# First batch's attention: unscaled probabilities, row factors applied to the output

## The chip, the cores and the metric

One NeuronCore of a Trainium2 chip runs the whole program. The metric is the device time of one execution in microseconds; the median of three executions of the kernel before is 1106.35 us (1105.39 to 1108.88).

## The reference

The inputs are `q`, `k`, `v` of shape (4, 8, 576, 64), a memory matrix `M_prev` and a vector `z_prev` per batch and head, a gate `beta` per head, and six feed-forward weights. For each of 4 batches and 8 heads:

```python
scores = scale * np.matmul(q, k.transpose(0, 1, 3, 2))     # causal mask follows
a = np.exp(scores - scores.max(-1, keepdims=True))
a /= a.sum(-1, keepdims=True) + 1e-09
local = np.matmul(a, v)
mem_out = einsum('bhsd,bhde->bhse', phi(q), M_prev) / (einsum('bhsd,bhd->bhs', phi(q), z_prev) + 1e-06)
out = g * mem_out + (1 - g) * local                        # g = sigmoid(beta), per head
```

The result, 2304 tokens by 512 features, goes through two feed-forward blocks: `((x@w1) * (x@w2)) @ w3 @ w_out`, and then `(sigmoid(x@w_gate) * (x@w_val)) @ w_out`. All of it is float32.

## The kernel before

**Work.** Heads go in pairs: two heads of 64 features fill the 128 partitions, four pairs (`NPAIR`) per batch. The 576 rows of a head are cut into five tiles of `T` = 116 rows. A batch's attention produces four tiles `Xt[p]` of shape 128 x 576 (features by tokens), each split into a rounded high part and a rest (`split_rows`, L310 to L313: a copy on ScalarE, a subtraction on VectorE or GpSimd). `ffn(b)` (L347) multiplies these with the weights in three-term products (`prod`, L300, matmuls at L302).

**Weights.** The weights arrive as 64-bit words and are turned into float32 on the chip, in half units of 128 x 512: `conv_step` (L180) with a scale (L199 on ScalarE or L201 on VectorE), a cast on ScalarE (L202), two integer operations on VectorE (L210, L211) and an integer add on GpSimd (L215); `split_step` (L239) then splits each half into its two parts (L311, L313) into a ring of `RING` = 5 slots. `w3` and `w_out` are first multiplied with each other (`prep`, L315: the `wps` matmuls).

**Stages.** The first stage runs attention of batch 0 beside the first four weight products (`start`, L781). `ffn(0)` follows, with attention of batch 1 woven in, and needs `Xt[0]` to `Xt[3]` for its `ab` matmuls; then `ffn(1)`, `ffn(2)` and `ffn(3)`, each with the attention of the next batch.

**Order.** `drive` (L750) takes one piece of attention for each piece of weight work by their costs. In the first stage only SyncE's queue has an order written by hand (L803); on the other engines a planner that simulates the time line at build time orders the instructions, with attention ahead by a priority of 400 (`AHEAD`). From `ffn(0)` on TensorE's order is the written one too (L814).

**Attention of batch 0, one pair.** For each row tile `i`: `s_part` makes the scores (L552) and VectorE adds the mask and takes the minimum (L557); `e_part` (L568) does the exponential on ScalarE with the row sum as a second result (L572, shown as the helper's L105); `n_part` (L577) adds 1e-9 to the two sums (L580), takes reciprocals (L581), and multiplies each head's probabilities by reciprocal and `1 - g` (L583; in batch 0 always on GpSimd, by `SHARE_N`). `t_part` (L595) transposes the result on TensorE against the identity (L613) and copies it out of PSUM (L629 or L631), three tiles behind (`LAG0`). `mem_steps` (L485) makes the scaled `phi(q)` (`mphi`; L495 and L504 on GpSimd), `qt_part` (L634) transposes it (L640, copies L646). `a_part` (L658) accumulates in one PSUM tile `o`: first the memory matrix times `qts` (L666), then the values times the transposed probabilities (L674, L681). `l_part` (L688) calls `tail` (L444), which splits the PSUM tile directly into `Xt[p]` while `xfree` is set, which holds for batch 0.

**PSUM.** `ps_f` has three buffers, shared by the feed-forward and weight products, by `qts` and by the wide transposes; `o` has one.

Of the kernel before, what the change touches and what calls it, by code (L numbers as in the profile page):

```python
# [7 lines left out]
F32 = mybir.dt.float32  # L8
# [42 lines left out]
def tile_attention_memory_ffn(  # L51
# [31 lines left out]
    idf = cp.tile([128, 128], F32, name="idf")  # L83
    idr = cp.tile([128, 128], F32R, name="idr")
    msk = cp.tile([T, SP], F32, name="msk")
# [363 lines left out]
    def attention(b, lag):  # L449
# [73 lines left out]

        sp = {}
        ots = {}
        qts = {}
        np_ = {"n": 0}

        def s_part(p, i, n):
            w = T * (i + 1)  # L530
            if n == 0:
                ps_ = []
                for hh in range(2):
                    name = f"p{b}_{p}_{i}_{hh}"
                    if first and np_["n"] % 2 == 0:
                        m = np_["n"] // 2 % P0
                        ps_.append(fp.tile([T, 2 * S], F32, tag=f"h{m}", name=name, bufs=1)[:, :SP])
                    else:
                        ps_.append(ap.tile([T, SP], F32, tag="p", name=name, bufs=PB))
                    np_["n"] += 1  # L540
                sp[p, i] = (ps_, ap.tile([T, 8], F32, tag="sm", name=f"sm{b}_{p}_{i}", bufs=6))
            ps_, sm = sp[p, i]
            c0, c1 = (0, w) if w <= 512 else ((0, SP // 2), (SP // 2, SP))[n]
# [24 lines left out]
        def e_part(p, i, hh):  # L568
            w = T * (i + 1)
            n = 1 if w > 512 else 0  # L570
            ps_, sm = sp[p, i]
            act_fn(  # L572
                out=ps_[hh][:, :w], in_=ps_[hh][:, :w], func=AF.Exp, scale=-1.0,
                bias=sm[:, 2 * hh + n : 2 * hh + n + 1], accum_out=sm[:, 4 + hh : 5 + hh],
            )

        def n_part(p, i):  # L577
            w = T * (i + 1)
            ps_, sm = sp[p, i]
            nc.vector.tensor_scalar(sm[:, 4:6], sm[:, 4:6], 1e-9, None, ALU.add)  # L580
            nc.vector.reciprocal(sm[:, 6:8], sm[:, 4:6])  # L581
            for hh in range(2):
                lower(SHARE_N).tensor_scalar(  # L583
                    ps_[hh][:, :w], ps_[hh][:, :w], sm[:, 6 + hh : 7 + hh],
                    omg[:T, 2 * p + hh : 2 * p + hh + 1], ALU.mult, ALU.mult,
                )
# [47 lines left out]
        def qt_part(p):  # L634
            qt = ap.tile([128, SP], F32, tag="qt", name=f"qts{b}_{p}")
            if first:
                for ts_ in (range(3), range(3, NT)):
# [7 lines left out]
                    w = T * len(ts_)  # L645
                    nc.scalar.copy(qt[:, ts_[0] * T : ts_[0] * T + w], ps[:, :w])  # L646
            else:
                ot = ps_o.tile([128, 1024], F32, tag="o", name=f"qt{b}_{p}")
# [9 lines left out]
        def a_part(p, part):  # L658
            X = 2 * T
            v_, m_ = pairs[p][1], pairs[p][2]  # L660
            halves_ = [slice(64 * hh, 64 * hh + 64) for hh in range(2)]
            if part == 0:
                ots[p] = ps_o.tile([128, 1024], F32, tag="o", name=f"o{b}_{p}")
# [7 lines left out]
            for j in range(2) if part == 0 else range(2, NT):  # L671
                if j < 2:
                    for hh, r in enumerate(halves_):
                        nc.tensor.matmul(  # L674
                            ot[r, XO + j * T : 512], v_[:, j, hh],
                            pq[:, hh, 2 * j : j + 2].rearrange("p a c -> p (a c)"),
                            start=False, stop=j == 1,
                        )
                q0 = max(2, j) * T
                for hh, r in enumerate(halves_):  # L680
# [3 lines left out]
                        if j < 4 else pt[:, hh, 3, 0, : S - 4 * T],  # L684
                        start=False, stop=j == NT - 1,
                    )

        def l_part(p):  # L688
            ot = ots.pop(p)[:, XO : XO + S]
            if state["xfree"]:  # L690
                tail(b, p, ot)
            else:
                xp = ap.tile([128, S], F32, tag="xp", name=f"xp{b}_{p}", bufs=4)
                nc.scalar.copy(xp, ot)
# [74 lines left out]
    def setup():  # L769
# [4 lines left out]
        nc.sync.dma_start(out=idf, in_=ident)  # L774
        nc.scalar.copy(idr, idf)
        nc.scalar.activation(out=g, in_=bt, func=AF.Exp, scale=-1.0)
# [110 lines left out]
```

## Time and profile before

| | us |
|---|---|
| median of three executions | 1106.35 |
| the profiled execution, its own time | 1107.55 |
| its span, first to last instruction | 1105.8 |
| TensorE busy | 1063.3 (96%) |
| VectorE busy | 533.9 (48%) |
| ScalarE busy | 468.7 (42%) |
| GpSimd busy | 326.9 (30%) |

The busy shares are means over stages with different limits. The batches after the first stage differ much from it: TensorE is busy throughout from 400 us on, while VectorE, ScalarE and GpSimd have most of their work before that. The change touches only what runs before about 128 us, so the views are read for that stretch. In the rows below PE is TensorE's matmul, PEld its weight load, DVE VectorE, ACT ScalarE, POOL GpSimd. The span starts 1.75 us short of the execution's own time.

### The profile page before, as it was taken

What the parts mean: (1) busy time and instruction counts of PE and PEld (TensorE: products, weight loads), DVE (VectorE), ACT (ScalarE), POOL (GpSimd) and SP (SyncE); (2) the same over time, 40 slices, a digit from 0 to 9 for tenths busy, and PEclk for the clock granted to TensorE, in tenths of its full rate; (3) what the DMA queues carried; (4) which work ended last, traced back from release to release, by engine and by line L of the source; (5) the groups of instructions that cost most, each with busy time, mean ns of one, the idle gap of its engine ahead of it and who ended that gap; (6) DMA issues with size and microseconds to landing.
All of it is one profiled execution on the core that took longest, in us unless ns stands there. A gap on an engine that the chain in (4) does not pass through costs nothing.

```text
span 1105.8 us, 19723 instructions
## 1 busy us (share of the span) xinstructions
PE 1063.3 (96%) x7616; PEld 950.7 (86%) x7616; DVE 533.9 (48%) x1251; ACT 468.7 (42%) x1030; POOL 326.9 (30%) x260
## 2 busy tenths in 40 slices
PE   6989798999999899999999999999999999999998
PEld 3555586887999789898999899889999899999998
DVE  7995888758788734553222415544222402212210
ACT  6776565645655633554322424454222412212210
POOL 5887565625666532222000202321000200000000
PEclk9999889999999899999999999999999999999999
DMA  8565568856888556443545454423554355454451
GB/s 271 167 207 186 178 219 287 272 188 211 268 298 305 206 193 220 149 151 128 171 156 171 153 171 159 163 85 134 163 167 160 101 164 189 154 171 171 154 174 61
DMA packets 69238, 201.76 MB, mean 182 GB/s; under 512 B 9624, under 2 KB 15896, under 8 KB 69144
## 3 DMA queue, kind: packets, MB, share of 16 engines
q1 hardware_dynamic: 69144, 200.50, 55.2%
q8 instruction: 60, 0.98, 0.4%
q14 instruction: 34, 0.28, 0.1%
HBM read 160.10 MB, written 40.37 MB: 181 GB/s over the span
## 4 chain that ended last, share of the span: by engine, by line
PE 75%; DVE 13%; POOL 4%; issue 4%; ACT 3%; DMA 2%; SPq 0%; DVEq 0%; POOLq 0%; ACTq 0%
PE gv L302 21%; PE ab L302 18%; PE ot L302 13%; PE xw L302 7%; PE s L552 4%; PE t L613 4%; DVE wraw L211 3%; PE o L681 3%; PE wps L302 3%; DVE wraw L210 2%; POOL wraw L215 2%; DVE p L557 1%; PE o L666 1%; POOL wslot L313 1%; DMA k<-wslot 1%
## 5 line engine op out<-in xcount | busy, mean ns | idle before, releaser
L302 PE MATMUL gv<-x,wslot 128*128 128x288 f32 x2304 | 308.2, 295 | 3.9 <-DVE hgraw L417 2.6
L302 PEld LDWEIGHTS gv<-x,wslot 128*128 128x128 f32 x2304 | 305.8, 188 | 5.8 <-DVE hgraw L417 4.2
L302 PE MATMUL ab<-x,wslot 128*128 128x288 f32 x1536 | 231.7, 303 | 0.0
L302 PEld LDWEIGHTS ab<-x,wslot 128*128 128x128 f32 x1536 | 210.6, 191 | 11.5 <-issue 8.3
L302 PE MATMUL ot<-hg,wslot 128*128 128x288 f32 x1152 | 166.1, 301 | 4.1 <-DVE hg L313 3.8
L583 POOL TENSOR_SCALAR p<-p,sm,omg 116x116 f32<-116x116 f32 (+4 forms) x100 | 100.6, 1010 | 224.2 <-DVE sm L581 159.8
L302 PEld LDWEIGHTS ot<-hg,wslot 128*128 128x128 f32 x1152 | 156.5, 190 | 10.4 <-issue 4.6
L215 POOL TENSOR_TENSOR wraw<-wraw,cr 128x512 int32<-128x512 int32 x76 | 112.1, 1489 | 65.7 <-DVE wraw L211 56.6
L105 ACT ACTIVATE p<-p,sm 116x116 f32<-116x116 f32 (+4 forms) x160 | 92.9, 582 | 73.4 <-DVE sm L557 68.5
L557 DVE CUSTOM_DVE_ANT_0 p<-s,msk 116x116 f32<-116x116 f32 (+4 forms) x160 | 68.2, 453 | 108.5 <-PE s L552 108.3
L417 DVE TENSOR_TENSOR hgraw<-gv,gsb 128x288 f32<-128x288 f32 x96 | 43.7, 455 | 141.5 <-PE gv L302 134.1
L302 PE MATMUL xw<-h,wslot 128*128 128x288 f32 x768 | 111.4, 299 | 0.2 <-DVE h L313 0.2
L302 PEld LDWEIGHTS xw<-h,wslot 128*128 128x128 f32 x768 | 103.1, 188 | 3.8 <-issue 2.5
L105 ACT ACTIVATE gsb<-gv 128x288 f32<-128x288 f32 x96 | 39.4, 410 | 112.0 <-PE gv L302 112.0
L613 PE MATMUL t<-idf,p 116*116 116x116 f32 x480 | 70.1, 276 | 14.0 <-DVE p L583 9.6
L613 PEld LDWEIGHTS t<-idf,p 116*116 116x116 f32 x480 | 54.8, 140 | 28.7 <-issue 16.5
L495 POOL TENSOR_TENSOR me<-mphi,z 116x640 f32<-116x640 f32 x16 | 25.4, 1589 | 176.0 <-issue 174.5
L373 DVE TENSOR_TENSOR hraw<-ab,asb 128x288 f32<-128x288 f32 x64 | 29.1, 456 | 70.1 <-PE ab L302 66.9
L202 ACT ACTIVATE cr<-r 128x512 int32<-128x512 uint32 x76 | 51.4, 676 | 27.0 <-POOL wraw L215 26.9
L211 DVE SCALAR_TENSOR_TENSOR wraw<-cy,wraw 128x512 int32<-128x512 int32 x76 | 62.3, 843 | 0.2
L313 POOL TENSOR_TENSOR wslot<-wraw,wslot 128x512 fp32r<-128x512 f32 x36 | 50.6, 1405 | 29.4 <-ACT wslot L311 28.8
L311 ACT CAST hg<-hgraw 128x576 fp32r<-128x576 f32 x48 | 32.3, 672 | 57.5 <-DVE hgraw L417 57.5
(79 smaller groups left out, 1139.0 us busy)
## 6 DMA issues: line engine op xcount, KB each, us to landing
wslot<-k SPq DMA_DIRECT2D x180, 512.0 KB, 3.6
k<-wslot SPq DMA_DIRECT2D x60, 512.0 KB, 5.6
r<-in_gv_dram SPq DMA_DIRECT2D x24, 512.0 KB, 4.9
qk<-in_qk_dram SPq DMA_DIRECT2D x32, 290.0 KB, 4.1
r<-in_w3t_dram SPq DMA_DIRECT2D x16, 512.0 KB, 4.0
r<-in_w_dram SPq DMA_DIRECT2D x16, 512.0 KB, 4.6
r<-in_o_dram SPq DMA_DIRECT2D x12, 512.0 KB, 5.4
qnr<-in_qn_dram SPq DMA_DIRECT2D x16, 320.0 KB, 3.3
```

Source lines behind the costliest of these rows:

```text
L105: ins = nc.scalar.activation(**kw)
L202: nc.scalar.activation(out=r, in_=w[:, :, 0].bitcast(U32), func=AF.Copy, scale=2.0**-29)
L211: nc.vector.scalar_tensor_tensor(z, y, -(2**31), z, ALU.bitwise_and, ALU.bitwise_or)
L215: nc.gpsimd.tensor_tensor(z, z, tmp["r"], ALU.add)
L302: nc.tensor.matmul(ps, w[:, wi, blk, :], x[:, xi, cols : cols + n], start=first and part == 0, stop=last and part == 2,)
L313: eng.tensor_sub(dst[:, 1], src, dst[:, 0].bitcast(F32))
L417: nc.vector.tensor_mul(hraw[:, c0 : c0 + HS], pss[1][:, :HS], asb)
L552: nc.tensor.matmul(os_[hh], q_[r, 0, i * T : (i + 1) * T], k_[r, 1, c0:c1], start=x == 0, stop=x == len(terms) - 1,)
L557: nc.vector.tensor_tensor_reduce(out=ps_[hh][:, c0:c1], in0=os_[hh], in1=msk[:, SP - w + c0 : SP - w + c1], scale=-0.125, scalar=3.0e38 if ...
L583: lower(SHARE_N).tensor_scalar(ps_[hh][:, :w], ps_[hh][:, :w], sm[:, 6 + hh : 7 + hh], omg[:T, 2 * p + hh : 2 * p + hh + 1], ALU.mult, ALU ...
L613: nc.tensor.transpose(tp[:T, c : c + T], src[hh][:, j * T : (j + 1) * T], idf[:T, :T])
L681: nc.tensor.matmul(ot[r, XO + q0 : XO + S], v_[:, j, hh], pt[:, hh, j].rearrange("p a c -> p (a c)")[:, q0 - X : S - X] if j < 4 else pt[: ...
```

## The change

In batch 0 the probabilities are transposed and used without their row factor. The ten row sums of a pair are collected in one small tile, get one addition and one reciprocal per pair, and are spread on GpSimd to a 116 x 640 tile that holds, for each row, the factor `(1-g)/sum` repeated over the head's 64 features. TensorE multiplies this with the identity (a transposition), ScalarE copies the result out of PSUM, VectorE multiplies the pair's output `o` with it, GpSimd adds the memory part, and `tail` splits the sum, now from SBUF. The memory part is no longer accumulated in `o`: `qt_part` multiplies `qts` by the memory matrix in two column halves through `ps_f`, and ScalarE copies the product over `qts`. An unused constant `idr` goes. The other batches keep their order of work.

```diff
-    idr = cp.tile([128, 128], F32R, name="idr")
@@ e_part
-                bias=sm[:, 2 * hh + n : 2 * hh + n + 1], accum_out=sm[:, 4 + hh : 5 + hh],
+                bias=sm[:, 2 * hh + n : 2 * hh + n + 1],
+                accum_out=sums[p][:, i, hh : hh + 1] if first else sm[:, 4 + hh : 5 + hh],
@@ n_part
+            if first:
+                if i == NT - 1:
+                    sums_ = sums[p]
+                    nc.vector.tensor_scalar(sums_, sums_, 1e-9, None, ALU.add)
+                    nc.vector.reciprocal(sums_, sums_)
+                    r = ap.tile([T, NT, 2, D], F32, tag="xp", name=f"spread{p}", bufs=4)
+                    nc.gpsimd.tensor_mul(
+                        r, sums_.unsqueeze(3).to_broadcast([T, NT, 2, D]),
+                        omg[:T, 2 * p : 2 * p + 2].unsqueeze(1).unsqueeze(3).to_broadcast([T, NT, 2, D]),
+                    )
+                    spread[p] = r.rearrange("p t a d -> p t (a d)")
+                return
@@ qt_part
+                m_ = pairs[p][2]
+                for c0, c1 in ((0, HS), (HS, S)):
+                    ps = ps_f.tile([128, 512], F32, tag="f", name=f"m{b}_{p}_{c0}")
+                    for hh in range(2):
+                        r = slice(64 * hh, 64 * hh + 64)
+                        nc.tensor.matmul(ps[r, :HS], m_[r], qt[r, c0:c1], start=True, stop=True)
+                    nc.scalar.copy(qt[:, c0:c1], ps[:, :HS])
@@ a_part
-            if part == 0:
+            if part == 0 and first:
+                ots[p] = ps_o.tile([128, 1024], F32, tag="o", name=f"o{b}_{p}")
+            elif part == 0:
...
-                            start=False, stop=j == 1,
+                            start=first and j == 0, stop=j == 1,
@@ l_part
-            if state["xfree"]:
+            if first:
+                x = ap.tile([128, NT * 2 * D], F32, tag="xp", name=f"xs{p}", bufs=4)[:, :S]
+                for ts_ in (range(2), range(2, NT)):
+                    c0, c1 = ts_[0] * T, min(S, (ts_[-1] + 1) * T)
+                    ps = ps_f.tile([128, 512], F32, tag="f", name=f"r{p}_{c0}")
+                    for n, t in enumerate(ts_):
+                        nc.tensor.matmul(
+                            ps[:, n * T : (n + 1) * T], spread[p][:, t], idf[:T, :T], start=True, stop=True
+                        )
+                    nc.scalar.copy(x[:, c0:c1], ps[:, : c1 - c0])
+                nc.vector.tensor_mul(x, ot, x)
+                nc.gpsimd.tensor_add(x, x, qts[p][:, :S])
+                tail(b, p, x)
+            elif state["xfree"]:
                 tail(b, p, ot)
@@ setup
-        nc.scalar.copy(idr, idf)
```

## Rows read from the trace of the kernel before

**Rows 1.** Stretches (us): busy time of PE, PEld, DVE, ACT, POOL; clock; DMA share, GB/s.

```profile
8.00:85.00 77.00, 68.84 (x277) 36.95 (x279) 72.54 (x169) 59.98 (x140) 64.03 (x54) 1.00 0.67 215
85.00:108.00 23.00, 22.68 (x127) 12.60 (x124) 15.07 (x48) 16.54 (x42) 17.93 (x18) 1.00 0.52 163
108.00:128.00 20.00, 20.00 (x108) 14.77 (x107) 14.01 (x25) 12.19 (x25) 10.60 (x10) 1.00 0.62 204
128.00:140.00 12.00, 2.64 (x15) 1.68 (x14) 12.00 (x24) 5.33 (x13) 7.04 (x6) 0.65 0.58 174
140.00:424.00 284.00, 268.99 (x1913) 242.42 (x1912) 201.98 (x399) 157.21 (x321) 152.79 (x109) 0.97 0.73 246
```

**Rows 2.** Chain of waits, 0 to 108 us, shares by engine and line.

```profile
by line: PE s L552 11.2%; DVE wraw L211 11.1%; PE wps L302 9.8%; DVE wraw L210 7.8%; DVE p L557 7.6%; PE t L613 5.7%; DMA r<-in_wo_dram 4.6%; issue 3.6%; POOL p L583 3.6%; DVE mphi L493 3.0%; POOL wraw L215 2.9%; PE o L681 2.5%; DVE wslot L
```

**Rows 3.** Groups by line, 0 to 108 us: busy us, mean ns | idle before, releasers.

```profile
L583 POOL TENSOR_SCALAR p<-p,sm,omg 116x116 f32<-116x116 f32 (+4 forms) x39 | 35.3, 913 | 17.9 <-DVE sm L581 17.3 <-ACT pt L631 0.6
L580 DVE TENSOR_SCALAR sm<-sm 116x2 f32<-116x2 f32 x20 | 5.7, 285 | 6.1 <-ACT p L105 6.1
L581 DVE RECIPROCAL sm<-sm 116x2 f32<-116x2 f32 x20 | 3.2, 158 | 0.3
L313 DVE TENSOR_TENSOR x<-o,x 128x576 fp32r<-128x576 f32 x3 | 2.2, 748 | 0.0
```

**Rows 4.** Same view: the operations nearest to those added.

```profile
L495 POOL TENSOR_TENSOR me<-mphi,z 116x640 f32<-116x640 f32 x4 | 6.2, 1550 | 0.8 <-DVE sm L580 0.8
L504 POOL TENSOR_TENSOR mphi<-mphi,mn 116x640 f32<-116x640 f32 x4 | 5.6, 1400 | 0.3 <-DVE sm L581 0.2 <-DVE mn L500 0.2
L640 PE MATMUL qt<-idf,mphi 116*128 116x116 f32 x20 | 3.4, 308 | 0.0
L646 ACT COPY qts<-qt 128x348 f32<-128x348 f32 (+1 forms) x8 | 2.8, 388 | 0.0
```

**Rows 5.** Same view: VectorE's SBUF work beside GpSimd's.

```profile
L215 POOL TENSOR_TENSOR wraw<-wraw,cr 128x512 int32<-128x512 int32 x20 | 28.8, 1452 | 5.2 <-DVE wraw L211 3.4 <-DVE sm L581 1.8
L211 DVE SCALAR_TENSOR_TENSOR wraw<-cy,wraw 128x512 int32<-128x512 int32 x20 | 20.1, 1011 | 0.2
L210 DVE TENSOR_SCALAR wraw<-cy 128x512 int32<-128x512 int32 x20 | 12.7, 644 | 0.2
L493 DVE SCALAR_TENSOR_TENSOR mphi<-qnr,me 116x640 f32<-116x640 f32 x4 | 5.3, 1332 | 0.0
```

**Rows 6.** By tile and by line: shortest/median/longest ns of those three VectorE groups.

```profile
L211 DVE SCALAR_TENSOR_TENSOR wraw<-cy,wraw x76: 666/682/1772, 9.7 to 388.4; 128x512 int32<-128x512 int32 x76
...
L210 DVE TENSOR_SCALAR wraw<-cy x76: 401/416/1744, 8.6 to 386.7; 128x512 int32<-128x512 int32 x76
...
L493 DVE SCALAR_TENSOR_TENSOR mphi<-qnr,me x4: 798/1400/1733, 10.7 to 90.3; 116x640 f32<-116x640 f32 x4
```

**Rows 7.** Time line, VectorE and GpSimd: start us, us, operation [idle before].

```profile
118.24 1.28 POOL L313 TENSOR_TENSOR wo<-wraw,wo 128x512 fp32r<-128x512 f32 x1 [0.43 <-ACT wo L311]
118.28 1.27 DVE L498 TENSOR_SCALAR mn<-mn 116x10 f32<-116x10 f32 x1
...
16.82 0.16 DVE L498 TENSOR_SCALAR mn<-mn 116x10 f32<-116x10 f32 x1
```

**Rows 8.** Time line, VectorE: additions that waited for an exponential.

```profile
89.52 0.47 DVE L580 TENSOR_SCALAR sm<-sm 116x2 f32<-116x2 f32 x1 [1.89 <-ACT p L105]
...
92.67 0.73 DVE L580 TENSOR_SCALAR sm<-sm 116x2 f32<-116x2 f32 x1 [0.82 <-ACT p L105]
```

**Rows 9.** Time line: the end of the first stage, last tail and first `ab` product.

```profile
121.55 0.64 ACT L311 CAST x<-o 128x576 fp32r<-128x576 f32 x1 [1.51 <-PE o L681]
...
125.18 3.01 PE L302 MATMUL wps<-wo,wslot 128*128 128x512 f32 x12
...
126.83 0.75 DVE L313 TENSOR_TENSOR x<-o,x 128x576 fp32r<-128x576 f32 x1
...
128.03 0.56 PE L302 MATMUL ab<-x,wslot 128*128 128x288 f32 x3
```

More of the change, by code (lines that the diff above doesn't have):

```diff
@@ L524, in attention @@
         sp = {}
+        sums = {}
+        spread = {}
         ots = {}
@@ L541, in s_part @@
                 sp[p, i] = (ps_, ap.tile([T, 8], F32, tag="sm", name=f"sm{b}_{p}_{i}", bufs=6))
+                if first and i == 0:
+                    sums[p] = ap.tile([T, NT, 2], F32, tag="sums", name=f"sums{p}", bufs=2)
             ps_, sm = sp[p, i]
@@ L684, in a_part @@
                         if j < 4 else pt[:, hh, 3, 0, : S - 4 * T],
-                        start=False, stop=j == NT - 1,
+                        start=first and j == 0, stop=j == NT - 1,
                     )
@@ L689, in l_part @@
             ot = ots.pop(p)[:, XO : XO + S]
-            if state["xfree"]:
+            if first:
[12 more added lines that the diff above has]
+            elif state["xfree"]:
                 tail(b, p, ot)
             else:
-                xp = ap.tile([128, S], F32, tag="xp", name=f"xp{b}_{p}", bufs=4)
+                xp = ap.tile([128, NT * 2 * D], F32, tag="xp", name=f"xp{b}_{p}", bufs=4)[:, :S]
                 nc.scalar.copy(xp, ot)
```

## The prediction, made before the change was run

> **What bounds the kernel now.** I read the stretches first, cut where the character of the work changes. From 8 to 85 us VectorE is busy 72.54 of 77 us, GpSimd 64.03, ScalarE 59.98; from 85 to 128 us the matmul row is full instead, and VectorE has idle time (15.07 of 23, 14.01 of 20) [rows 1]. A full matmul row overstates TensorE, since matmuls overlap, but nothing else in that stretch is close to full. Behind it lies a hole: between 128 and 140 us TensorE works 2.64 of 12 us while VectorE works all 12, and the granted clock of that stretch is 0.65, a mean between its two levels of 1.2 and 2.4 GHz. The stretch from 140 to 424 us, the rest of `ffn(0)`, is not touched by the change; what is gained or lost by 128 us is carried into it, if nothing swallows it on the way.
>
> The chain of waits to 108 us says the same: no line has more than 11.2%, and VectorE's weight conversions (L211, L210) and score step (L557) stand beside TensorE's scores, weight products and transpositions. GpSimd's scaling, the work that is removed, has 3.6% of 108 us there, 3.9 us [rows 2], though it is GpSimd's largest group with 35.3 us [rows 3]. So most of what goes was off the path, and the gain has to come from VectorE and from waits.
>
> **What goes, by engine.** GpSimd: 39 recorded scalings, 35.3 us. VectorE: 20 additions and 20 reciprocals, 5.7 + 3.2 = 8.9 us [rows 3]. The four `o` products with the memory matrix are moved, not removed. ScalarE loses one copy of 0.3 us at start-up, which I count as nothing.
>
> **What comes.** Per pair, VectorE gets one addition and one reciprocal on 116 x 10; I take the means of the 116 x 2 forms, since so few columns cost mostly the start: 4 x (0.285 + 0.158) = 1.8 us. It gets one multiplication of 128 x 576 out of PSUM; the tail's subtraction has that shape and source, 0.748 us: 4 x 0.748 = 3.0 us [rows 3]. The tail's subtraction now reads SBUF alone; I leave its time unchanged. VectorE's own sum: 1.8 + 3.0 - 8.9 = -4.1 us.
>
> GpSimd gets four spreading multiplications (nearest: L495, 1.55 us) and four additions of 128 x 576 (nearest: L504, 1.40 us) [rows 4]: 11.8 us. Its load falls by 23.5 us. In itself that is worth nothing where GpSimd isn't last.
>
> TensorE gets 20 transpositions of the shape of L640, 3.4 us in all [rows 4]; the moved products keep their columns. ScalarE gets 16 copies like L646, 16 x 0.388 = 6.2 us. It was busy 59.98 of 77 us, so the copies are hidden behind VectorE there; were that cover gone, three pairs' share, 4.7 us, would be paid. SyncE's queue gets no DMA and keeps its order; the memory matrix is read a little earlier, but the load of `v`, which stands ahead of it in that queue, is released as before.
>
> **Where the two engines meet.** The trace shows VectorE held up while GpSimd works: an addition on 116 x 10 took 1.27 us beside a GpSimd subtraction of 1.28 us, and 0.16 us elsewhere [rows 7]. Three VectorE groups of the first 108 us, held against their shortest run, lost 20 x (1.011 - 0.666) + 20 x (0.644 - 0.401) + 4 x (1.332 - 0.798) = 6.9 + 4.9 + 2.1 = 13.9 us [rows 5, 6]. Beside them GpSimd's four large groups worked 35.3 + 28.8 + 6.2 + 5.6 = 75.9 us [rows 3 to 5], so VectorE lost 0.18 us per us of GpSimd work. By that rate the removed scalings gave back 6.4 us and the new ones cost 2.1 us. But on the time line the long VectorE runs lie mostly beside GpSimd's two-input operations, and the scalings have one input. I take half of the credit: 2.1 - 3.2 = -1.1 us. The ends: full credit, -4.3 us; no credit and every new GpSimd operation holding up VectorE for the 1.27 - 0.16 = 1.11 us of rows 7, +8.9 us.
>
> The Trainium skill, "SBUF — State Buffer", section "SBUF: two separate sides", calls this an exclusive lock on a port pair, held for a whole instruction, and has VectorE lose it when it reads two SBUF tensors or runs in its two-port mode. By it the scalings would have locked like the rest, so the credit would be whole; but the same rule speaks against the change, since the new GpSimd operations lock as well and the tail's subtraction now reads two SBUF tensors. The pair of rows at 118 us agrees with it.
>
> **The sum.** VectorE: -4.1 - 1.1 = -5.2 us over four pairs. Three pairs lie where VectorE is full, -3.9 us. After 85 us TensorE is full: it gets two pairs' transpositions, +1.7 us. There, VectorE waited twice in its queue with an addition for an exponential, 1.89 and 0.82 us [rows 8], with the next tile's score step behind it, on which that tile's exponential and then TensorE wait; those additions are gone: -2.7 us. What is late next there is TensorE's own order.
>
> The last pair's end grows. Before, the output goes to a ScalarE copy at 121.55 and a VectorE subtraction at 126.83 that ends 127.58, while TensorE has 24 weight products to do until 128 and then starts `ab` [rows 9]: the tail had 0.45 us to spare. After, a VectorE product (0.75) and a GpSimd addition (1.40) come in between, in queues that also hold conversions: a subtraction or conversion behind them waits too. Without delay in a queue it ends earlier than the old one; with the old delay of 4.6 us it ends 2.1 us later, less the spare 0.45. I take +1.0 us between 0 and 1.7.
>
> Together: -3.9 + 1.7 - 2.7 + 1.0 = -3.9 us, against the profiled execution's own 1107.55 us (its span of 1105.8 and 1.75 around it). The median, 1106.35, lies 1.2 us lower; I forecast for it: 1106.35 - 3.9 = 1102.5 us, 0.35% less. About 0.3%, 3.3 us, is what a measurement of this kernel can tell from no change, so this forecast lies at that edge.
>
> **Rivals.** *GpSimd was the real bound.* With full credit VectorE's sum is -4.1 - 4.3 = -8.4, three quarters -6.3, and the total -6.3 + 1.7 - 2.7 + 1.0 = -6.3. If TensorE's waits behind the scaling also matter, the chain's 3.9 us [rows 2] go in addition: -10.2 us, 1096.1. For: GpSimd was busy 64.03 of 77 us [rows 1], and the scaling stood between each exponential and its transpositions. Against: GpSimd itself waited 17.3 us for VectorE's reciprocals [rows 3].
>
> *The locks eat it.* In the stretch to 85 us, six of the eight new two-input GpSimd operations each start just ahead of a VectorE operation. No credit, 8.9 us of cost: VectorE -4.1 + 8.9 = +4.8, three quarters +3.6; and the waits of rows 8 stay, now behind locks: 3.6 + 1.7 + 1.0 = +6.3 us, 1112.7. It decides from about 1.3 us of lock wait per pair more than before, where the total crosses zero (-3.9 against 3 x 1.3). For: rows 7, and that GpSimd keeps a full queue of conversions. Against: eight operations beside 28 of that kind that were there before [rows 4, 5] and cost VectorE far less each. By the rule of the Trainium skill named above, this price would be paid by each VectorE operation that loses the lock, and the removed ones would pay theirs back.
>
> *The hole swallows it.* From 128 to 140 us VectorE is full and TensorE waits [rows 1]. If the hole's end hangs on VectorE's conversions, and those on DMA and ring slots rather than on the first stage, `ab` starts earlier only to wait longer: -3.9 becomes about -1 us, 1105.3. For: TensorE idles 9.4 us there. Against: every conversion is issued behind the same queue and would move with it.
>
> *The planner reorders.* The first stage's order comes from a simulation at build time, so the new instructions can shift others: a weight product of 3.0 us [rows 9] put before a score step or after it. One such shift either way, +-3 us, is in the range.
>
> **Chances.** Forecast (between -2 and -6 us) 0.40, of which a little over half lies beyond 3.3 us; GpSimd the bound 0.22; locks 0.20; hole 0.14; that the engines don't do what the change says, with the order so altered that none of these fits, 0.04. Faster by over 0.3%: 0.22 + 0.23 + 0.02 = 0.47. Slower by over 0.3%: 0.20 + 0.02 and 0.01 of the hole's, 0.23. Within: 0.30. The range reaches from GpSimd's case, 1096.1, less 1 for its scatter, to just under the locks' full price: 1095 to 1112.
>
> **What would show it.** Right: GpSimd's busy time in the first stage falls by about 23 us, VectorE's by about 5; L211's and L210's means fall a little; the first `ab` product starts near 124 instead of 128 us; from 140 us on everything is shifted alike. Wrong: L211 or L210 longer on average than 1.011 and 0.644 us (locks); the first `ab` product earlier by 8 us or more (GpSimd); the shift present at the first `ab` product and gone at 140 us (hole); the first `ab` product late, with TensorE waiting for the last tail's GpSimd addition, which would make the +1.0 term wrong.

## The result and the profile after

The kernel after takes **1112.96 us** (median of 5; 1110.49 to 1114.84), the kernel before 1106.35: a ratio of 1.0054 [1.0033, 1.0074]. It is slower, by 6.6 us; the forecast was 1102.5 us, and the time lies 1 us above the range. The profiled execution took 1110.49 us (span 1108.7), against 1107.55 (1105.8) before, so the profile shows 2.9 of the 6.6 us.

The stretches of the kernel after, in the columns of [rows 1]:

```profile
8.00:85.00 77.00, 72.00 (x288) 37.83 (x289) 72.72 (x150) 63.44 (x152) 44.96 (x32) 1.00 0.67 222
85.00:108.00 23.00, 22.69 (x122) 13.83 (x122) 13.52 (x35) 15.15 (x37) 10.27 (x8) 1.00 0.39 127
108.00:128.00 20.00, 19.16 (x111) 14.01 (x110) 11.28 (x22) 11.77 (x28) 9.36 (x8) 1.00 0.49 163
128.00:140.00 12.00, 9.02 (x39) 6.49 (x39) 12.00 (x20) 5.34 (x12) 8.38 (x6) 0.86 0.56 166
140.00:424.00 284.00, 265.05 (x1889) 238.01 (x1890) 210.28 (x410) 159.69 (x327) 156.08 (x112) 0.98 0.74 248
```

To 85 us GpSimd's busy time falls as forecast, from 64.03 to 44.96 us with new work in it, but VectorE's does not fall at all (72.54 to 72.72); it falls from 85 to 128 us, by 4.28 us, part of which is work that now comes after 128 us. From 128 to 140 us TensorE, which waited there before, has 9.02 us of work, most of it work that was done by 128 us before. The lateness is still there at the first `xw` matmul of `ffn(0)` (the product that follows `ab`), before and after:

```profile
245.76 0.56 PE L302 MATMUL xw<-h,wslot 128*128 128x288 f32 x3
```

```profile
249.81 0.56 PE L301 MATMUL xw<-h,wslot 128*128 128x288 f32 x3
```

In all 20 profiles of this study the end of the span follows the first `xw` matmul by 858.5 to 860.3 us, so what a variant does to the time is settled in the first 250 us.

The groups of 0 to 108 us that answer to [rows 4, 5]; L210, L209, L214, L494 are L211, L210, L215, L495 of before, L592 makes the spread factors, L729 adds the memory part:

```profile
L210 DVE SCALAR_TENSOR_TENSOR wraw<-cy,wraw 128x512 int32<-128x512 int32 x20 | 20.6, 1038 | 0.2
...
L214 POOL TENSOR_TENSOR wraw<-wraw,cr 128x512 int32<-128x512 int32 x20 | 28.8, 1443 | 28.8 <-DVE wraw L210 18.8 <-DVE mn L498 6.8 <-ACT cr L201 1.4
L209 DVE TENSOR_SCALAR wraw<-cy 128x512 int32<-128x512 int32 x20 | 14.6, 738 | 0.3 <-ACT cy L198 0.2
...
L494 POOL TENSOR_TENSOR me<-mphi,z 116x640 f32<-116x640 f32 x4 | 6.3, 1585 | 2.6 <-DVE mphi L492 2.6
L592 POOL TENSOR_TENSOR spread<-sums,omg 116x640 f32<-116x640 f32 x4 | 5.6, 1397 | 1.5 <-DVE sums L590 1.1 <-ACT qts L672 0.4
...
L729 POOL TENSOR_TENSOR xs<-xs,qts 128x576 f32<-128x576 f32 x2 | 3.0, 1480 | 2.9 <-DVE xs L728 2.8
```

The means that should have fallen rose, 1011 to 1038 and 644 to 738 ns, and GpSimd now waits 18.8 us for L210 (3.4 us before). A weight product is here one PSUM tile `wps` of 12 matmuls (the prediction calls a single matmul so). The first stage makes eight of them, two in each of the four steps of `start`: the first pass, with the first half of `w_out`; the second pass, with the second half, follows in `ffn(0)`. On TensorE's time line the end of the stage, which answers to [rows 9], looks like this: first the 8th product of before, then the kernel after, with VectorE's last tail put between.

```profile
115.84 3.02 PE L302 MATMUL wps<-wo,wslot 128*128 128x512 f32 x12
```

```profile
120.60 7.20 PE L301 MATMUL wps<-wo,wslot 128*128 128x512 f32 x29
...
123.79 0.76 DVE L312 TENSOR_TENSOR x<-xs,x 128x576 fp32r<-128x576 f32 x1 [2.25 <-ACT x L310]
...
127.99 0.97 PE L301 MATMUL wps<-wo,wslot 128*128 128x512 f32 x3 [0.19 <-POOL wo L312]
...
130.30 0.50 PE L301 MATMUL wps<-wo,wslot 128*128 128x512 f32 x1 [1.34 <-DVE wo L312]
...
133.29 3.42 PE L301 MATMUL wps<-wo,wslot 128*128 128x512 f32 x12
...
136.55 0.56 PE L301 MATMUL ab<-x,wslot 128*128 128x288 f32 x3
```

The last tail is ready at 124.55 us, 3 us earlier than before. But the 7th and 8th weight products, done by 118.9 us before, start at 120.60, when attention is over; the second half of `w_out`, whose buffers they hold, is converted only behind them, and TensorE waits for it at 127.99 and 130.30. The first `ab` starts at 136.55 instead of 128.03 us. Part of that is given back in the hole, which VectorE's conversions fill in both kernels; 4.0 us are left at `xw`. The start of `ab` alone doesn't tell the time of a variant: in z_wo_before (point 6), which is faster than the kernel before, it lies at 138.53 us.

### The profile page after: what moved, and what is told of

The parts are those of the page before. It is cut to its first block, busy times and chain, and to the rows that moved or that the text cites. A ratio compares the mean times of both kernels' runs of the same rounds, so it can differ in the third digit from the quotient of the medians.

```text
span 1108.7 us, 19741 instructions
## 1 busy us (share of the span) xinstructions
PE 1071.8 (97%) x7656; PEld 956.0 (86%) x7656; DVE 538.6 (49%) x1223; ACT 473.9 (43%) x1045; POOL 303.6 (27%) x228
## 4 chain that ended last, share of the span: by engine, by line
PE 73%; DVE 15%; issue 4%; DMA 3%; ACT 3%; POOL 2%; SPq 0%; POOLq 0%; DVEq 0%; ACTq 0%
PE gv L301 21%; PE ab L301 18%; PE ot L301 13%; PE xw L301 7%; PE s L555 4%; DVE wraw L210 3%; PE t L631 3%; PE o L709 3%; DVE wraw L209 3%; DVE p L560 2%; DMA k<-wslot 2%; DVE wslot L312 2%; DVE cy L200 1%; PE wps L301 1%; PE o L694 1%
## 5 line engine op out<-in xcount | busy, mean ns | idle before, releaser
L214 POOL TENSOR_TENSOR wraw<-wraw,cr 128x512 int32<-128x512 int32 x76 | 113.2, 1502 | 90.7 <-DVE wraw L210 68.6
L601 POOL TENSOR_SCALAR p<-p,sm,omg 116x116 f32<-116x116 f32 (+4 forms) x60 | 63.5, 1058 | 196.8 <-DVE sm L599 131.4
L494 POOL TENSOR_TENSOR me<-mphi,z 116x640 f32<-116x640 f32 x16 | 25.6, 1597 | 177.1 <-issue 174.5
L210 DVE SCALAR_TENSOR_TENSOR wraw<-cy,wraw 128x512 int32<-128x512 int32 x76 | 62.3, 843 | 0.2
L310 ACT CAST hg<-hgraw 128x576 fp32r<-128x576 f32 x48 | 32.4, 674 | 57.5 <-DVE hgraw L416 57.5
```

Of the source, the lines that this page charges most:

```text
L210: nc.vector.scalar_tensor_tensor(z, y, -(2**31), z, ALU.bitwise_and, ALU.bitwise_or)
L214: nc.gpsimd.tensor_tensor(z, z, tmp["r"], ALU.add)
L601: lower(SHARE_N).tensor_scalar(ps_[hh][:, :w], ps_[hh][:, :w], sm[:, 6 + hh : 7 + hh], omg[:T, 2 * p + hh : 2 * p + hh + 1], ALU.mult, ALU ...
```

## The experiments

All ratios are to the kernel before on the same chip, with 95% intervals; half widths of differences are the root of the summed squares. The kernels come in the order in which the reasons were taken apart.

**1. The removal alone, and the change without its spread factors.** x_rem is the kernel before with

```diff
 def n_part(p, i):
+    if first:
+        return
```

and x_nospread the kernel after with

```diff
-                    r = ap.tile([T, NT, 2, D], F32, tag="xp", name=f"spread{p}", bufs=4)
-                    nc.gpsimd.tensor_mul(
...
-                for ts_ in (range(2), range(2, NT)):
...
-                    nc.scalar.copy(x[:, c0:c1], ps[:, : c1 - c0])
-                nc.vector.tensor_mul(x, ot, x)
+                nc.vector.tensor_copy(x, ot)
```

> The kernel before with batch 0's additions, reciprocals and scalings left out and nothing in their place (batch 0 is not normalised): what the removal alone is worth. Order theory (the loss is that the planner puts the last two weight products behind the last attention work, plus TensorE's share of the new products): without new work the removal gains, 1099 to 1104 us, first ab product near 124 us. Rival, the removal is worth nothing because GpSimd and VectorE's small operations were hidden: 1105 to 1108 us.

> The changed kernel without the row factors (no spreading on GpSimd, no 20 products and 8 copies; VectorE copies o instead of multiplying it; batch 0 is not normalised): the memory part alone in its new place. TensorE theory (the 20 factor products cost 5.6 us of TensorE at two passes each, and push the last weight products behind): 1102 to 1106 us. Lock theory (new two-input GpSimd operations hold VectorE up): half of them stay, so about half of the loss, 1109 to 1110 us.

Measured: x_rem 1105.08 us, **0.9974 [0.9958, 0.9990]**; x_nospread 1106.00 us, 0.9988 [0.9977, 0.9999]. Taking the whole scaling away, with nothing in its place, is worth 2.9 us at this interleaving. The stretch from 8 us to the first weight product of the second pass, before and in x_rem:

```profile
8.00:121.45 113.45, 104.98 (x475) 59.24 (x475) 95.07 (x232) 84.76 (x199) 89.01 (x78) 1.00 0.64 207
```

```profile
8.00:120.30 112.30, 108.80 (x474) 62.13 (x473) 83.02 (x189) 84.24 (x198) 52.10 (x38) 0.97 0.62 201
```

VectorE's two conversion groups in x_rem, 0 to 108 us:

```profile
L211 DVE SCALAR_TENSOR_TENSOR wraw<-cy,wraw 128x512 int32<-128x512 int32 x20 | 15.6, 789 | 0.2
L210 DVE TENSOR_SCALAR wraw<-cy 128x512 int32<-128x512 int32 x20 | 12.2, 616 | 0.0
```

VectorE gives back 12.05 us (95.07 to 83.02) and GpSimd 36.9, and the stage ends 1.15 us earlier. Of VectorE's time 5.0 us come from the conversions themselves (20.1 to 15.6 and 12.7 to 12.2, against [rows 5]): the removed scalings did hold it up. What closes is TensorE's idle time, 8.47 to 3.50 us. Its row gets 3.8 us longer with the same products, and the granted clock of the stretch is 0.97, by estimate (3% of 112.3 us) 3.4 us of full-speed time lost. So VectorE's load did not set the length of this stage, at this interleaving: after 12 us of relief TensorE's row is nearly all of it, in part at the lower clock. x_rem was run at one interleaving only, and point 4 shows how much that choice weighs; what the removal is worth at another is not known.

**2. Multiplications or products?** Of the 6.6 us, x_nospread leaves none, so in this interleaving they come with the spread factors: four large GpSimd multiplications, or the factor products with their copies, and the order planned for either. v_one makes the factors once, for one query tile, in one small multiplication of 0.46 us:

```diff
-                    r = ap.tile([T, NT, 2, D], F32, tag="xp", name=f"spread{p}", bufs=4)
-                    nc.gpsimd.tensor_mul(
...
+                    if not spread:
+                        spread["r"] = ap.tile([T, 2 * D], F32, tag="spc", name="spread", bufs=1)
+                        nc.gpsimd.tensor_mul(
...
-                            ps[:, n * T : (n + 1) * T], spread[p][:, t], idf[:T, :T], start=True, stop=True
+                            ps[:, n * T : (n + 1) * T], spread["r"], idf[:T, :T], start=True, stop=True
```

v_mul has the second half of x_nospread's edit, from `for ts_` on, and keeps the multiplications.

> The kernel after, with the spread factors made once, from the first pair's sums and for one query tile, and used for all pairs and tiles: the row factors of all other tiles are left out. 20 factor products per batch, their copies and VectorE's product stay, and TensorE's planned order is the one of after but for two score steps; three of the four large GpSimd multiplications, 4.2 us, and their hold on VectorE are gone. If the GpSimd multiplications and their locks are the loss: 1106 to 1109 us (0.998 to 1.002), as x_nospread. If the factor products with the order that goes with them are: 1110 to 1114 us (1.003 to 1.007).

> The reverse: the kernel after with all four GpSimd spreading multiplications but without the factor products, their ScalarE copies and the row factors on the output (a plain copy takes the place of VectorE's product; the normalisation is left out). TensorE's planned order is nearly that of x_nospread. If the locks are the loss: 1110 to 1114 us (1.003 to 1.007). If the factor products with their order are: 1105 to 1108 us (0.998 to 1.001).

Measured: v_one 1109.34 us, **1.0020 [1.0008, 1.0032]**; v_mul 1108.76 us, **1.0015 [1.0003, 1.0026]**. Neither theory has it alone. The multiplications cost 0.27% (+-0.16) without the products and 0.34% (+-0.24) with them; the products with what comes along cost 0.32% (+-0.16) and 0.39% (+-0.24). Each alone they make 0.59%, together 0.66%, so the two nearly add up. VectorE's conversions, 0 to 108 us, in x_nospread, v_mul, v_one and x_frac125 (point 4: all of the change, woven otherwise):

```profile
L210 DVE SCALAR_TENSOR_TENSOR wraw<-cy,wraw 128x512 int32<-128x512 int32 x20 | 18.1, 912 | 0.2
L209 DVE TENSOR_SCALAR wraw<-cy 128x512 int32<-128x512 int32 x20 | 13.5, 686 | 0.6 <-ACT cy L198 0.6
```

```profile
L210 DVE SCALAR_TENSOR_TENSOR wraw<-cy,wraw 128x512 int32<-128x512 int32 x20 | 19.6, 989 | 0.2
L209 DVE TENSOR_SCALAR wraw<-cy 128x512 int32<-128x512 int32 x20 | 14.0, 706 | 0.4 <-ACT cy L198 0.4
```

```profile
L210 DVE SCALAR_TENSOR_TENSOR wraw<-cy,wraw 128x512 int32<-128x512 int32 x20 | 19.1, 958 | 0.2
L209 DVE TENSOR_SCALAR wraw<-cy 128x512 int32<-128x512 int32 x20 | 13.9, 702 | 1.4 <-POOL wslot L312 0.9 <-ACT cy L198 0.5
```

```profile
L210 DVE SCALAR_TENSOR_TENSOR wraw<-cy,wraw 128x512 int32<-128x512 int32 x20 | 18.8, 946 | 0.2
L209 DVE TENSOR_SCALAR wraw<-cy 128x512 int32<-128x512 int32 x20 | 13.6, 689 | 1.2 <-ACT cy L198 0.8 <-POOL wslot L312 0.3
```

With the multiplications L210 and L209 take 19.6 + 14.0 us instead of 18.1 + 13.5 (2.0 more, v_mul), and in after 20.6 + 14.6 instead of 19.1 + 13.9 (2.2 more than v_one). In this interleaving 4 to 6 us of two-input GpSimd work go with about 2 us more on VectorE, some 0.4 to 0.5 us per us, where the 35.3 us of scalings cost these groups 5.0 us, 0.14 per us. That is no price of the operation: x_frac125 has the same instructions as after, with three of the four multiplications, 3.8 us, before 108 us, and its two groups take 18.8 + 13.6 us, 2.8 less than after and 0.8 more than x_nospread, 0.2 us per us. How long VectorE is held up depends on what the order puts beside what, and no run shows how much of the multiplications' 0.3% is hold-up and how much is order.

**3. TensorE's own time for the products.** x_tr makes each factor product a transposition; y_tr125 does so at the interleaving of 1.25 of point 4.

```diff
-                        nc.tensor.matmul(
-                            ps[:, n * T : (n + 1) * T], spread[p][:, t], idf[:T, :T], start=True, stop=True
-                        )
+                        nc.tensor.transpose(ps[:, n * T : (n + 1) * T], spread[p][:, t], idf[:T, :T])
```

> The changed kernel with the 20 factor products issued as transpositions, one pass each, nothing else. TensorE theory: 10 passes per pair become 5, 2.8 us of TensorE in all, so 1110 us; if only the order counts, it is as the changed kernel, 1112 to 1113 us, since the planned order still has the last two weight products at the end. Lock theory: 1112 to 1113 us.

> The changed kernel at 1.25 with the 20 factor products as transpositions: does TensorE's extra work count once the order is mended? If it does, 2.8 us less of it give 1103 to 1105 us against 1106.3 without; if VectorE or its queue sets the end of the stage, 1105 to 1107 us.

Measured: x_tr 1114.11 us, 1.0056 [1.0040, 1.0072]; y_tr125 1.0013 [1.0003, 1.0023], against 0.9994 for its own pair x_frac125. The groups of products on TensorE, 0 to 121 us: the memory products of before, then after and x_tr:

```profile
L666 PE MATMUL o<-qts,ms 64*64 64x232 f32 (+1 forms) x32 | 6.2, 493 | 0.0
```

```profile
L671 PE MATMUL m<-qts,ms 64*64 64x288 f32 x32 | 7.4, 492 | 0.0
L724 PE MATMUL r<-idf,spread 116*128 116x116 f32 x40 | 6.4, 291 | 0.0
```

```profile
L724 PE MATMUL r<-idf,spread 116*128 116x116 f32 x20 | 3.7, 281 | 0.2 <-POOL p L601 0.2
```

A factor product leaves two records where the transposition leaves one, and they take 6.4 us instead of 3.7. The moved memory products take 7.4 us instead of 6.2. In the row of the stretch up to the second pass they show: the kernel after has 112.24 us of it busy, 7.26 more than before, and 2.51 us less idle, which is the 4.75 us by which its second pass starts later.

```profile
8.00:126.20 118.20, 112.24 (x512) 64.98 (x513) 95.71 (x205) 89.08 (x213) 62.80 (x45) 1.00 0.59 193
```

Yet halving the records gains nothing that shows: x_tr stands 0.02% (+-0.26) above after, which alone would hardly exclude a gain of 2.7 us (0.24%), but y_tr125 is 0.19% (+-0.13) slower than its pair. So TensorE's time for them alone hardly accounts for what they cost; the copies on ScalarE and the order are left, and no run decides between these. In x_tr's profile the clock was also at its lower level within the first stage, so this one profile can't be read as a pure saving of 2.7 us.

**4. The order.** The planner weaves weight products and attention by costs; the factor of the first stage, 1.0, sets how far attention may run ahead.

```diff
-    drive(start(), chain(a0, atts[1]), 42.4 * NPREP + 8 * WAIT, ATOT, 1.0, most=9)
+    drive(start(), chain(a0, atts[1]), 42.4 * NPREP + 8 * WAIT, ATOT, 1.25, most=9)
```

x_frac125 and v_f11 (1.1) are the kernel after, y_bfrac125 and y_bfrac09 (0.9) the kernel before.

> The changed kernel with one number of the interleaving altered (the share by which attention runs ahead of the weight products in the first stage, 1.0 to 1.25): the same instructions, the last weight products now planned beside attention, none behind it. Order theory: first ab product back near 128 us, 1102 to 1107 us. TensorE theory and lock theory: the same work and the same locks, 1111 to 1114 us.

> The kernel after, whole, with the interleaving factor of the first stage at 1.1, between 1.0 (1.0054) and 1.25 (0.9994); the planned order has the 7th weight product ahead of the last output products and the 8th behind. If the loss grows with how far the weight products fall behind attention: between the two, 1107 to 1112 us (1.000 to 1.005). If the order does not decide: as after, 1111 to 1114 us.

> The kernel before with the same altered number of the interleaving, 1.25: the control. Order theory, strict form (the change itself is worth about nothing or a small gain, and its loss comes from where the last weight products stand): the order of before was already good, so this stays within 1104 to 1108 us. Rival, 1.25 is simply a better number for any kernel and hides a real loss of the change: 1100 to 1103 us.

> The kernel before with that number at 0.9: nothing of the change in it, but the last weight product and most of the one ahead of it now planned behind the last attention work. Order theory: slower by most of the change's loss, 1109 to 1113 us, first ab product after 132 us. If the change's own instructions make its loss: 1105 to 1108 us.

Measured: x_frac125 1106.32 us, **0.9994 [0.9985, 1.0002]**; v_f11 1.0037 [1.0019, 1.0054], between, but not told apart from after; y_bfrac125 0.9998 [0.9987, 1.0009]; y_bfrac09 1116.28 us, **1.0091 [1.0074, 1.0108]**. The same instructions as in after, woven otherwise, lose nothing; and the kernel before, with nothing of the change, loses more than the change does when its weight products are pushed back. TensorE's weight products at the end of the stage, y_bfrac09 and then x_frac125:

```profile
125.55 5.63 PE L302 MATMUL wps<-wo,wslot 128*128 128x512 f32 x22
131.36 0.96 PE L302 MATMUL wps<-wo,wslot 128*128 128x512 f32 x3 [0.18 <-POOL wo L313]
...
133.67 0.50 PE L302 MATMUL wps<-wo,wslot 128*128 128x512 f32 x1 [1.34 <-DVE wo L313]
...
139.98 0.56 PE L302 MATMUL ab<-x,wslot 128*128 128x288 f32 x3
```

```profile
109.66 3.02 PE L301 MATMUL wps<-wo,wslot 128*128 128x512 f32 x12
...
114.80 3.04 PE L301 MATMUL wps<-wo,wslot 128*128 128x512 f32 x12
...
124.08 2.33 PE L301 MATMUL wps<-wo,wslot 128*128 128x512 f32 x9
...
130.59 0.56 PE L301 MATMUL ab<-x,wslot 128*128 128x288 f32 x3
```

y_bfrac09 shows the picture of after, down to the waits of 0.18 and 1.34 us for `w_out`. In x_frac125 the 7th and 8th products run at 109.66 and 114.80 us, before the last outputs; the second pass starts at 124.08 and has no wait. The stretches of x_frac125 to its second pass and on to its first `xw`, then the second of these in after:

```profile
8.00:124.08 116.08, 108.99 (x513) 63.97 (x513) 100.71 (x211) 90.88 (x219) 66.45 (x47) 0.97 0.64 208
124.08:244.68 120.60, 111.42 (x725) 94.26 (x725) 94.20 (x205) 68.54 (x149) 64.91 (x48) 0.93 0.71 233
```

```profile
126.20:249.81 123.61, 111.06 (x725) 92.36 (x724) 100.49 (x211) 71.27 (x155) 69.73 (x52) 0.94 0.73 237
```

Of the 5.1 us by which x_frac125 is ahead of after at `xw`, 2.1 are there when the second pass starts; the other 3.0 come behind it, where VectorE has 6.3 us less to do; in the first stage it has 5.0 us more (100.71 against 95.71). Its second pass even starts 2.6 us later than that of before, and nothing is lost.

**5. Is it the last two products?** In w_p3 the matmuls of the 7th and 8th products get a higher priority, so that they go ahead of some of the last outputs; the rest of TensorE's planned order stays. w_bp3 is the same edit on the kernel before. y_dve125 (x_frac125 with the memory part added on VectorE) belongs beside them as a try to unload GpSimd.

```diff
-                prod(ps, slot(s), m, wot[4 * p + m], 0, m == 0, m == 3, n=DM)
+                if p == 0 and g >= 3:
+                    w_ = slot(s)
+                    with tc.high_priority(offset=600):
+                        prod(ps, w_, m, wot[4 * p + m], 0, m == 0, m == 3, n=DM)
...
```

```diff
-                nc.gpsimd.tensor_add(x, x, qts[p][:, :S])
+                nc.vector.tensor_add(x, x, qts[p][:, :S])
```

> The kernel after, with one edit: the matmuls of the first pass's last pair of weight products get a higher priority, so that TensorE's planned order ends ... o, 7th product, o, 8th product instead of ... o, 7th, 8th product; everything ahead of them keeps its place. If the place of the last two products behind the last output products is the loss: the first weight product of the second pass starts at 123 to 125 us instead of 126.2, and the time is 1107 to 1110 us (0.998 to 1.003). If the loss sits earlier, in products two to six, which interleaving 1.25 moved too: it stays at 1111 to 1114 us (1.004 to 1.007).

> Control: the kernel before with the same edit, which moves its 8th product ahead of the last output products. Either theory: 1104 to 1107 us (0.998 to 1.001).

> The changed kernel at 1.25 with the addition of the memory part on VectorE in place of GpSimd: four GpSimd operations fewer (5.8 us) and four VectorE operations more (3 us), and a hop less in the tail. Lock theory: VectorE is held up less, 1103 to 1105 us. If VectorE's own load counts more than the hop and the locks: 1106 to 1109 us.

Measured: w_p3 1112.58 us, 1.0051 [1.0037, 1.0065]; w_bp3 0.9995 [0.9983, 1.0008]; y_dve125 1.0032 [1.0020, 1.0044]. The place of the last two products, which the time line makes the plain suspect, does not give the loss back by itself. The 6th product of after, then the 6th, 7th and 8th of w_p3, and TensorE's row of w_p3 from 60 to 70 us (busy time, granted clock, DMA share, GB/s):

```profile
111.64 3.03 PE L301 MATMUL wps<-wo,wslot 128*128 128x512 f32 x12
```

```profile
114.11 3.03 PE L301 MATMUL wps<-wo,wslot 128*128 128x512 f32 x12
...
120.26 2.99 PE L301 MATMUL wps<-wo,wslot 128*128 128x512 f32 x12
...
124.11 3.06 PE L301 MATMUL wps<-wo,wslot 128*128 128x512 f32 x12
```

```profile
60.00:70.00 10.00, 10.00 (x26) 0.50 0.50 153
```

This execution is 2.5 us behind after by the 6th product, with the clock at its lower level from 60 to 70 us. Counted from the 6th, the 7th comes 2.8 us sooner than in after, so the edit does what it should; the first `ab` comes 1 us earlier all the same, and the time, a median of six executions, stays. Nor does a lag before them decide: by 85 us before and x_frac125 have four products of the first pass done, after three and y_bfrac09 two, but x_nospread and z_wo_before have three and lose nothing. The addition is better on GpSimd, at 1.25.

**6. The wait for `w_out`.** Its second half gets other buffers, which are free earlier, and no longer those of the first half:

```diff
-            t = fp.tile([128, 2, S], F32R, tag=f"h{8 + m % 4}", name=f"wo{m}", bufs=1)
+            t = fp.tile([128, 2, S], F32R, tag=f"h{8 + m if m < 4 else m}", name=f"wo{m}", bufs=1)
```

z_wo_after and z_wo_before are the two kernels with this edit, z_wo_frac125 and z_wo_bfrac125 have 1.25 as well, w_p3_wo is w_p3 with it.

> The changed kernel with one buffer choice altered: the second half of w_out is split into the buffers of probability tiles that are free by then, not into those that the last weight product of the first pass still reads. The planned order keeps the last two weight products behind the last attention work. If the loss is that this conversion is exposed behind them: 1104 to 1108 us, no wait between the 8th and the 9th weight product. If it is the late weight products and TensorE's extra work alone: 1109 to 1112 us. Lock theory: 1112 to 1114 us.

> The same buffer choice in the kernel before, the control: there the conversion ran beside the last attention work, so 1105 to 1108 us if it was hidden; 1101 to 1104 us if VectorE's queue near 120 us, where the conversion and the last tail meet, set the end of the stage.

> The changed kernel with both, the interleaving at 1.25 and the buffer choice: with the order mended the conversion is beside other work, so 1104 to 1107 us; if the two add up, 1101 to 1104 us and the best of all.

> The kernel before with both, the interleaving at 1.25 and the buffer choice: the control of the fastest kernel. If the change is worth nothing once order and conversion are mended: 1100 to 1103 us, as the changed kernel with both. If the removal of the scalings then pays: 1103 to 1106 us, as the kernel before with the buffer choice alone.

> The kernel after with the same edit and with the second half of w_out in buffers of its own choice (as in z_wo_after, 1.0024). If both causes are separate, the gains add: 1.0024 less what w_p3 gains on 1.0054. If the last two products cost only by delaying the buffers of w_out's second half, the edit gains nothing here: 1.001 to 1.004.

Measured: z_wo_after 1.0024 [1.0012, 1.0035], z_wo_before 0.9973 [0.9962, 0.9985], z_wo_frac125 1101.52 us, **0.9945 [0.9927, 0.9962]**, z_wo_bfrac125 1.0016 [1.0008, 1.0025], w_p3_wo 1.0002 [0.9991, 1.0014]. The conversion of `w_out` costs both kernels 0.3%, so it isn't the difference between them (1.0024 against 0.9973 is still 0.51%). With it out of the way the place of the last two products counts for 0.22% (+-0.16); without, it was 0.03% (+-0.25), which does not exclude as much. The fastest is the kernel after with both edits, 0.55% faster than before; before with both is slower. So an interleaving fits one set of instructions and not another, and the worth of the change depends on it. Against the kernel before with the same edits it is +0.54% (+-0.20) as first measured, -0.04% (+-0.14) at 1.25, +0.51% (+-0.16) with the other buffers and -0.71% (+-0.19) with both. The best of each, z_wo_frac125 and z_wo_before, are 0.28% (+-0.21) apart, in favour of the change.

## Why the prediction was wrong

**The failed step** is the first one, "the gain has to come from VectorE and from waits", with the factor of three quarters by which VectorE's time became time of the kernel. By the prediction's terms the removal is worth (8.9 + 3.2) x 3/4 + 2.7 = 11.8 us; x_rem measured 2.9 (0.26%). The amount was right: VectorE gave back 12.05 us where 12.1 stood in the sum. That the amounts agree is partly luck: the conversions of [rows 5] and the removed operations gave more, and other subtractions got longer (L313 into `wslot`, 866 to 1251 ns on average to 108 us). But a full VectorE row to 85 us was read as a bound, and the row of TensorE beside it, 68.84 of 77 us [rows 1], was left out of that reading. From 8 us to the second pass TensorE had 8.47 us idle in 113.45; taken at its word, that row leaves no more than this to gain, and 2.9 us came. A busy row can be longer than its work needs (11 matmuls of a weight product take 4.79 us from 41.96 us in the kernel before, 12 take 3.04 from 56.26, at a granted clock of 1.00 both times), so 8.47 us is a guide and not a proven limit. Nearly all of the miss stands here: 8.9 of about 10 us.

**What was added was priced about right in sum**: (1.8 + 3.0 + 2.1) x 3/4 + 1.7 + 1.0 = 7.9 us; from x_rem to after it is 0.80% (+-0.26), 8.9 us. Its parts were not, so that the sum is close is luck:

- *Locks.* Forecast: a gain of 1.1 us. The credit is there and larger than the half taken (5.0 us in two groups against 3.2 in three). In after more than all of it is gone again: the two groups stand at 20.6 + 14.6 us against 20.1 + 12.7 before, 2.4 us longer. The multiplications (four in v_mul, three of them in v_one) are worth 0.27 to 0.34% of the time, 3.0 to 3.8 us; the whole lock charge had been 2.1. The rival "the locks eat it" has the right sign and nearly the right time (1112.7), the latter by luck: its price per operation was too high, the multiplications with whatever locks they bring are about half of the loss, and the waits of [rows 8], which it kept, went. The Trainium skill, "SBUF — State Buffer", section "SBUF: two separate sides", has the pair held as an exclusive lock for a whole instruction, whichever engine starts first. The runs agree that VectorE's conversions get shorter when GpSimd work goes (35.3 us of it, 5.0 us shorter); that L209, with one input, is hit as well (644 to 738 ns) is in line with its clause on the two-port mode, but no run here shows the mode. The rates differ, 0.14 us per us for scalings and 0.4 to 0.5 for multiplications at the interleaving of 1.0, but the 0.2 of x_frac125 shows that they are rates of an order and not of an operation. The tail's subtraction, which now reads two SBUF tensors, took 1.19 and 1.33 us in the first two pairs and 0.75 and 0.76 in the last two, against 0.748 before; the prediction left it unchanged.
- *TensorE +1.7.* The factor products were sized by the transpositions of L640; all four pairs take 6.4 us, not 3.4, and the moved memory products 1.2 us more than before. But halving the former gained nothing that shows, so the 0.32 to 0.39% (3.5 to 4.3 us) that they bring are more likely in their copies or in the order, which the prediction costed at nothing; this is argued, as the two were not run apart.
- *The last tail +1.0.* Wrong: it is ready 3.0 us earlier than before and nothing waits for it. The prediction took 24 matmuls of weight products to stand beside it; when it starts, 48 are undone.
- *The waits of rows 8, -2.7.* They went (what is left of such waits to 108 us is 2.1 us, before the addition of each pair, against 6.1 in [rows 3]), and attention got ahead by some 4 us: its last scores of batch 0 start at 100.32 us instead of 104.72. It bought nothing by itself, since the work that attention passed, the weight products, is what the next stage starts on.
- *The order.* "One such shift either way, +-3 us", with 0.04 for an order so altered that nothing fits. At 1.25 the same instructions are 0.60% (+-0.22) faster (6.6 us, the whole loss), and at 0.9 the kernel before is 0.91% slower, 10 us. The order is worth more than any term of the sum and deserved a case of its own.
- *The hole.* In part: of 8.5 us at the first `ab` product 4.0 are left at `xw`.

What stays open: what the removal is worth at another interleaving; how much of the multiplications' cost is hold-up on VectorE and how much order; how the cost of the factor products splits between ScalarE's copies and the order; why 1.25 suits the kernel after and not the one before; and the step from x_rem to x_nospread (the moved memory products, the plain copy and GpSimd's addition), 0.14%, which its interval (+-0.19) does not tell from nothing.

## What to carry to other kernels

Before time saved on the fullest helper engine is counted, look at how much TensorE idles in that stretch: by its row that is about the most that relief beside it can bring without a new order, and here 2.9 of 8.5 us came. Don't carry a rate of hold-up between two engines, in us per us, from one order to another: the same instructions, woven in two ways, left VectorE's two conversion groups at 35.2 and 32.4 us. Where a planner weaves the order, run a change at two or three weavings before judging it, and the kernel before with it: against before at the same setting this change stood between 0.54% slower and 0.71% faster.

## What the runs showed of the hardware

In several variants TensorE's clock was at its lower level within the first stage, where before and after had 1.00 throughout. In x_tr (stretch, busy time of PE, granted clock, DMA share, GB/s):

```profile
40.00:50.00 10.00, 9.04 (x35) 0.68 0.56 196
50.00:60.00 10.00, 7.94 (x48) 1.00 0.86 284
60.00:70.00 10.00, 10.00 (x24) 0.50 0.50 149
```

From 60 to 70 us the matmul row is full and the granted clock is 0.50, which is the level of 1.2 GHz; from 50 to 60 us TensorE was busy 7.94 us at 1.00. A stretch at the lower level makes a row look fuller without any more work, as in x_rem, whose row grew 3.8 us with the same products. A lower clock over the whole execution is not the cause of the loss: the mean granted clock of the five executions of after is 0.989, that of 139 executions of before 0.985.
